# Pair 0 of a pooled attention: rows of maxima through TensorE instead of DMA, k's first rows on ScalarE's queue, one shared last query tile

## The chip, the cores and the metric

The kernel runs on one core of one Trainium2 chip. The metric is the device time of one execution in microseconds (us), as the median of several runs. One execution is an attention followed by two feed-forward layers; the change lies in the first 3% of it.

## The reference, cut to what matters

```python
# q, k, v: (4, 8, 1152, 64) float32
q_pool = q.reshape(B, H, S // 2, 2, D).mean(axis=3)          # 576 query rows per head
scores = scale * np.matmul(q_pool, k.transpose(0, 1, 3, 2))  # 576 x 1152
scores = scores - np.max(scores, axis=-1, keepdims=True)
attn = np.exp(scores)
attn = attn / (np.sum(attn, axis=-1, keepdims=True) + 1e-09)
x = np.matmul(attn, v)                # 32 heads, then laid out as 2304 x 512
h = x @ w_in;  x = (h - np.tanh(h)) @ w_out                  # d_ff 2048
h = x @ w_in2; x = (h / (1.0 + np.exp(-1.702 * h))) @ w_out2
```

## The kernel before, in words

**Pairs and steps.** The 32 heads go in 16 pairs. A pair's two heads lie on partitions 0 to 63 and 64 to 127 of its q and k tiles (64 dimensions each). The main loop counts steps `g`: 9 key tiles of 128 keys for each head, so 18 steps for a pair; steps 0 to 8 belong to head 0 of pair 0, steps 9 to 17 to its head 1, and step 18 opens pair 1. `scores(g)` makes the scores of one key tile, transposed (128 keys by 576 queries, in two PSUM banks), with four matmuls: L400 takes the high part and L401 the correction. For L401 the moving operand `q3` has a 65th row, the negated row of maxima of this head, so that the maximum is subtracted inside the matmul. No scores of a head can start before its `q3` row is there. ScalarE then takes exp of the scores (L406, `pf`), and in two steps of three a second time, rounded (L416, `ph`); VectorE or GpSimd takes their difference (`pl`, L424). `pv(g - 3)` multiplies with v three steps later (L446, six matmuls; in every third step L436, two unrounded ones).

**Maxima.** For a row of maxima, TensorE makes the scores the other way round (128 queries by 1152 keys) only to reduce them: VectorE's `tensor_reduce` leaves one negated maximum per query in a column of `mt`. For the pairs from 1 on, both heads stand in one block-diagonal query tile `bdqs`, and each of nine query tiles is done in two halves of the keys (`max_tile`, L324 and L328), one half in each of 18 steps, starting at step 4 for pair 1. From step 3 on the PSUM pool of these tiles has one buffer. For pair 0 (`first_max`, L340 and L344) head 0's five query tiles (four of 128 rows, one of 64) are done with all 1152 keys at once before the loop, then three of head 1's; head 1's last two tiles follow as halves in steps 0 to 3. `max_rows` (L347) turns the columns of `mt` into a row: a 32x32 transpose on VectorE, then four DMAs (three of SP's queue, one of ScalarE's) into row 64 of `q3`. Head 1's row is made at step 4.

**The opening.** q and k of pair 0 are loaded in halves of 64 partitions (L258, L263: 64 x 1152 float32, 288 KB each), all on SP's queue in the order q low, k low, q high, k high; the third key tiles of v (`prep_v_whole`, 96 KB) go first on ScalarE's queue. VectorE sums the query pairs (L543), ScalarE and GpSimd round k (`k_high`, L551 and L553), GpSimd takes the remainders (`k_low`, L557). `keep_warm` (L585) issues matmuls of zeros whose result nobody reads.

**Order.** The scheduler is off (`tc.manual_schedule`): every engine runs its instructions in the order in which the code issues them. A PSUM pool that closes hands its banks on: the first scores wait for the last reader of the opening's pools. What happens beside the steps is set by tables: `max_at` gives the maxima's steps, `opening` the work of the first pairs by (pair offset, step): `refill_v`, `refill_row` (L234, L238: fixed rows of ones and zeros copied to the second buffer set), `prep_kh`, `prep_bdq`, `prep_qh` (ScalarE), `prep_kl` (GpSimd), `stack` (six DMAs).

Of the kernel before, what the change touches and what calls it, by code (L numbers as in the profile page):

```python
# [28 lines left out]
def tile_pooled_attention_two_moe(  # L29
# [181 lines left out]
    def attention(ctx: ExitStack):  # L211
# [119 lines left out]
        def first_max(s, j, x, pool, parts, n):  # L331
            d = pairs[0]
            r = slice(64 * s, 64 * s + 64)
            a1, _, q2, _ = stacks[0]
            lhs, rhs = (q2, a1) if s == 0 else (d["qh"], d["kh"])
            m = min(128, SP - 128 * j)
            mx = pool.tile([128, parts, 512], F32, tag="mx", name="mx")
            for a in range(parts):
# [4 lines left out]
            c = 16 * x + 5 * s + j
            nc.vector.tensor_reduce(  # L344
                d["mt"][0:m, c:c + 1], mx[0:m, :, 0:n], AX.XY, ALU.max, negate=True)

        def max_rows(p, s, queues=(nc.sync,) * 4):  # L347
# [13 lines left out]
            for a in range(4):  # L361
                if p == 0:
                    m, j = a, 5 * s
                else:
                    j = 0 if s == 0 else 4 if a >= 2 else 5
                    m = 4 * j + a - 18 * s
# [181 lines left out]
        def k_high(eng, out, r, x):  # L548
            o, i = half(out, r, x), half(kraw[0], r, x)
            if eng is nc.scalar:  # L550
                eng.activation(o, i, AF.Copy)  # L551
            else:
                eng.tensor_scalar(  # L553
                    out=o, in0=i, scalar1=1.0, scalar2=1.0, op0=ALU.mult, op1=ALU.mult)
# [14 lines left out]
        nc.scalar.activation(q2[high], d0["qs"][low], AF.Copy)  # L569
        k_high(nc.scalar, d0["kh"], high, 0)  # L570
        k_high(nc.scalar, d0["kh"], high, 1)
        refill_v(1)
        nc.scalar.activation(d0["qh"][high], d0["qs"][high], AF.Copy)
        refill_row(1)
# [341 lines left out]
```

## Time and profile before

| | us |
|---|---|
| median of 3 runs | 1306.44 (1306.07 to 1310.09) |
| the profiled execution, its own time | 1304.36 |
| its span in the profile | 1302.6 |
| TensorE busy in the span | 1286.1 (99%) |
| VectorE, ScalarE, GpSimd busy | 990.2 (76%), 752.7 (58%), 361.9 (28%) |

The span is what the profile covers; 1.76 us of the execution's own time lie outside of it. TensorE is busy nearly throughout, but its busy time in the opening includes the matmuls of zeros, so the opening has to be read row by row: when a row starts, how long it takes, and what released it.

### The profile page before, as it was taken

The numbers are of one execution on the slowest core, as the hardware profiler recorded it, in microseconds if no ns is written. First come the engines' busy times: TensorE is split into PE (matmuls) and PEld (weight loads), VectorE is DVE, ScalarE is ACT, GpSimd is POOL, SyncE is SP. The second block draws the span as 40 slices with busy tenths as digits, with TensorE's granted clock in tenths as the row PEclk, the third lists the DMA queues.
The fourth block names the chain that finished last, engine by engine and source line by source line (L and its number), as shares of the span: only waits on it lengthen the run. The fifth ranks groups of instructions, "written<-read, shape, count | busy, mean of one in ns | idle before, by whom it ended". The sixth has DMA issues, their size and how long they took to land.

```text
span 1302.6 us, 18879 instructions
## 1 busy us (share of the span) xinstructions
PE 1286.1 (99%) x7027; PEld 1148.7 (88%) x7027; DVE 990.2 (76%) x1278; ACT 752.7 (58%) x1153; POOL 361.9 (28%) x272
## 2 busy tenths in 40 slices
PE   8999999999999999999999999999999999999998
PEld 5999999999999998878889889889889889889887
DVE  7777787887878888999999999999943645645433
ACT  5777777777777777776766665665543322322211
POOL 6533333333434333234333332332100100100000
PEclk9999999999999999999999999999999999999999
DMA  6776666676766630211111111111211111111012
GB/s 180 184 177 172 168 168 155 166 186 167 176 167 171 146 89 23 74 49 33 50 33 49 49 33 48 34 33 49 66 36 46 49 33 50 49 33 33 25 41 81
DMA packets 58682, 116.24 MB, mean 89 GB/s; under 512 B 24928, under 2 KB 29024, under 8 KB 58592
## 3 DMA queue, kind: packets, MB, share of 16 engines
q1 hardware_dynamic: 58172, 114.96, 34.1%
q8 instruction: 55, 0.90, 0.3%
q14 instruction: 35, 0.29, 0.1%
q10 hardware_dynamic: 420, 0.10, 0.0%
HBM read 66.58 MB, written 4.79 MB: 55 GB/s over the span
## 4 chain that ended last, share of the span: by engine, by line
PE 81%; DVE 12%; ACT 3%; issue 2%; DMA 1%; POOL 1%; DVEq 0%; SPq 0%; ACTq 0%; POOLq 0%
PE y L802 25%; PE h L707 23%; PE pv L446 10%; PE pv L436 6%; PE mx L324 5%; PE sc L401 5%; PE sc L400 5%; DVE wt L137 1%; DVE gg L765 1%; DVE mt L328 1%; DVE wt L143 1%; DVE mt L344 1%; DVE wt L157 1%; DVE xb L815 1%; DVE wt L150 1%
## 5 line engine op out<-in xcount | busy, mean ns | idle before, releaser
L328 DVE TENSOR_REDUCE mt<-mx 128x1 fp32r<-128x576 f32 x270 | 203.6, 754 | 81.4 <-PE mx L324 77.1
L406 ACT ACTIVATE pf<-sc 128x576 f32<-128x576 f32 x288 | 188.4, 655 | 124.8 <-PE sc L401 110.3
L707 PE MATMUL h<-hl,big 128*128 128x512 f32 (+1 forms) x940 | 211.6, 377 | 0.0
L707 PEld LDWEIGHTS h<-hl,big 128*128 128x128 f32 x940 | 174.0, 188 | 28.6
L400 PE MATMUL sc<-q,big 128*128 128x288 f32 x576 | 183.4, 332 | 0.8 <-DVE mt L344 0.7
L802 PE MATMUL y<-g,big 128*128 128x512 f32 (+1 forms) x780 | 176.6, 369 | 3.3 <-ACT xb L813 1.7
L802 PE MATMUL y<-big,g 128*128 128x512 f32 x702 | 172.2, 390 | 0.0
L802 PEld LDWEIGHTS y<-g,big 128*128 128x128 f32 x780 | 141.9, 188 | 25.0 <-POOL g L719 3.4
L401 PE MATMUL sc<-q,a 65*128 65x288 f32 x576 | 163.7, 298 | 0.0
L719 POOL TENSOR_TENSOR g<-gg,g 128x1024 fp32r<-128x1024 f32 (+1 forms) x39 | 85.8, 2200 | 273.0 <-ACT g L717 273.0
L717 ACT ACTIVATE g<-gg 128x1024 fp32r<-128x1024 f32 (+1 forms) x80 | 78.0, 974 | 140.5 <-DVE gg L778 74.8
L802 PEld LDWEIGHTS y<-big,g 128*128 128x128 f32 x702 | 131.6, 188 | 27.2
L446 PE MATMUL pv<-ph,big 128*128 128x288 f32 x768 | 141.7, 295 | 0.5 <-ACT u L452 0.5
L815 DVE TENSOR_TENSOR xb<-xb,y 128x512 f32<-128x512 f32 (+1 forms) x114 | 72.2, 655 | 87.3 <-PE y L802 87.3
L424 DVE TENSOR_TENSOR pl<-pf,ph 128x576 fp32r<-128x576 f32 x159 | 132.5, 834 | 2.2 <-ACT ph L416 1.5
L707 PE MATMUL h<-hl,w 128*128 128x512 f32 (+1 forms) x564 | 127.0, 377 | 0.0
L165 POOL TENSOR_TENSOR big<-wt,big 128x512 fp32r<-128x512 f32 x46 | 65.2, 1424 | 217.5 <-ACT big L164 217.5
L416 ACT ACTIVATE ph<-sc 128x576 fp32r<-128x576 f32 x188 | 122.8, 653 | 0.0
L707 PEld LDWEIGHTS h<-hl,w 128*128 128x128 f32 x564 | 104.4, 188 | 17.1
L324 PE MATMUL mx<-kh,big 128*128 128x288 f32 x540 | 117.4, 299 | 1.6 <-DVE mt L328 1.4
L446 PEld LDWEIGHTS pv<-ph,big 128*128 128x128 f32 x768 | 116.1, 188 | 1.0 <-issue 0.9
L400 PEld LDWEIGHTS sc<-q,big 128*128 128x128 f32 x576 | 109.3, 190 | 7.1 <-POOL big L385 1.1
(101 smaller groups left out, 2146.5 us busy)
## 6 DMA issues: line engine op xcount, KB each, us to landing
raw<-in_moe_w_in_dram SPq DMA_DIRECT2D x32, 512.0 KB
raw<-in_moe_w_out_dram SPq DMA_DIRECT2D x32, 512.0 KB
big<-kh SPq DMA_DIRECT2D x31, 288.0 KB
q<-qh SPq DMA_DIRECT2D x62, 144.0 KB
big<-kl SPq DMA_DIRECT2D x31, 288.0 KB
a<-kh SPq DMA_DIRECT2D x31, 288.0 KB
kr<-in_k_dram SPq DMA_DIRECT2D x15, 576.0 KB
qr<-in_q_dram SPq DMA_DIRECT2D x15, 576.0 KB
```

What stands on the lines that cost most here:

```text
L324: nc.tensor.matmul(mx[:, a, 0:n], bdqs[p % 2][:, 128 * j:128 * j + 128], d["kh"][:, k0:k0 + n], start=True, stop=True)
L328: nc.vector.tensor_reduce(d["mt"][:, c:c + 1], mx[:, :, 0:n], AX.XY, ALU.max, negate=True)
L400: nc.tensor.matmul(sc[:, x, 0:HB], a1[:, ks], q2[:, xs], start=True, stop=False)
L401: nc.tensor.matmul(sc[:, x, 0:HB], a2[:, ks], q3[:, xs], start=False, stop=True)
L406: nc.scalar.activation(both(pf), sc[:, :, 0:HB], AF.Exp, scale=SCALE)
L416: nc.scalar.activation(both(ph), sc[:, :, 0:HB], AF.Exp, scale=SCALE)
L424: eng.tensor_tensor(pl, pf, f32(ph[:]), op=ALU.subtract)
L446: nc.tensor.matmul(accs[hd][x], w[:, t, :], r[:, x * HB:(x + 1) * HB], start=(t == 0 and n == 0), stop=(t == KT - 1 and n == 2))
L707: nc.tensor.matmul(hb[:, j, 0:TBS[b]], wi[:, c, w, :], x[r][c], start=(k == 0), stop=(k == 3 * NKC - 1))
L719: eng.tensor_tensor(gt[:, :, 1, :], g, f32(gt[:, :, 0, :]), op=ALU.subtract)
L802: nc.tensor.matmul(ys[m][:, 0:w], lhsT, rhs, start=(fp == 0 and k == 0), stop=(fp == 1 and k == 5))
L815: nc.vector.tensor_add(dst, dst, ys[m][:, 0:w])
```

## The change

Pair 0 alone is changed.

- `first_max` writes its maxima into spare columns of `bdqs[0]` (`first_mt`) instead of `mt`. `first_row` makes the row with five matmuls against an identity (which GpSimd writes with `affine_select` into `bdqs[0]`), into the PSUM tile of the zeros (`warm`); ScalarE copies 512 elements of it to `q3`, VectorE the last 64. No transposes and no DMAs are left for pair 0's rows.
- Head 1's and head 0's last 64 queries share one tile of 128 (j = 4), through the block-diagonal `bdqs[1]` and both heads' `kh`.
- Before the loop stand head 0's five tiles, its row, and one half tile of head 1; head 1's other seven half tiles go to steps 0 (two) to 5, its row to step 6 (`second_row`).
- k low is issued on ScalarE's queue; `prep_v_whole` comes after it there.
- Pair 1's first eight half tiles move from steps 4 to 11 to steps 6, 7, 8, 8, 9, 10, 11, 11; where a step has two jobs, the second stands behind the step's `pv`.
- Half of a1's rounding goes from GpSimd to VectorE, `q3`'s remainder (`q_low`) from VectorE to GpSimd. `kh` gets its low half too, for the shared tile.
- `prep_kh` of pair 1, `refill_row` and `refill_v` go from before the loop into steps 1 to 8; `prep_kl`, `sum_q`, `prep_bdq`, `prep_qh`, `prep_ql` and `stack` of pair 1 move one to three steps back.
- `keep_warm` issues 7 + 4 matmuls instead of 11 + 5 + 7.

```diff
-        def refill_v(i):
-            for old, new in zip((*vt[0], vfs[0]), (*vt[i], vfs[i])):
-                nc.scalar.activation(new[:, :, D:128], old[:, :, D:128], AF.Copy)
+        def refill_v(i, n):
+            old, new = [(*vt[x], vfs[x])[n] for x in (0, i)]
+            nc.scalar.activation(new[:, :, D:128], old[:, :, D:128], AF.Copy)
...
+        ident = bdqs[0][:, 0:128]
+        first_mt = bdqs[0][:, 128:288]
+
+        def first_max(s, j, x, pool, parts, n, banks=2):
             d = pairs[0]
+            a1, _, q2, _ = stacks[0]
             r = slice(64 * s, 64 * s + 64)
-            a1, _, q2, _ = stacks[0]
             lhs, rhs = (q2, a1) if s == 0 else (d["qh"], d["kh"])
-            m = min(128, SP - 128 * j)
-            mx = pool.tile([128, parts, 512], F32, tag="mx", name="mx")
+            q0 = 128 * j
+            if j == 4:
+                r, lhs, rhs, q0 = slice(0, 128), bdqs[1], d["kh"], 512
+            mx = pool.tile([128, banks, 512], F32, tag="mx", name="mx")
...
+            c = 64 + 16 * x + 5 * s + j
+            return lambda: nc.vector.tensor_reduce(
+                first_mt[:, c:c + 1], mx[:, 0:parts, 0:n], AX.XY, ALU.max, negate=True)
+
+        def first_row(s, row, js):
+            q3 = stacks[s][3]
+            for j in js:
+                c = 4 if j == 4 else 5 * s + j
+                nc.tensor.matmul(
+                    row[:, 128 * j:128 * j + 128], first_mt[:, c:c + 128], ident,
                     start=True, stop=True)
...
+            if 3 in js:
+                nc.scalar.activation(q3[D:D + 1, 0:512], row[D:D + 1, 0:512], AF.Copy)
+            if 4 in js:
+                nc.vector.tensor_copy(
+                    q3[D:D + 1, 512:SP], row[D:D + 1, 512 + 64 * s:SP + 64 * s])
+
+        def second_row():
+            nc.vector.tensor_tensor(
+                first_mt[:, 69:73], f32(first_mt[:, 69:73]), f32(first_mt[:, 85:89]), op=ALU.min)
+            first_row(1, flat(ps_mx.tile([128, 2, 512], F32, tag="mx", name="mx")), range(5))
...
         load_q(0, low)
-        load_k(0, low)
+        load_k(0, low, nc.scalar)
         load_q(0, high)
+        prep_v_whole(0, 0, nc.scalar)
         load_k(0, high)
         load_v(0, 0)
-        prep_v_whole(0, 0, nc.scalar)
...
         nc.gpsimd.memset(f32(bdqs[0][:]), 0.0)
+        nc.gpsimd.affine_select(
+            out=ident, in_=f32(ident), compare_op=ALU.not_equal, fill=1.0, base=0,
+            pattern=[[-1, 128]], channel_multiplier=1)
...
         q_sum(nc.vector, q2[low], low)
-        k_high(nc.scalar, a1, low, 0)
-        k_high(nc.gpsimd, a1, low, 1)
+        k_high(a1, low, 0)
+        nc.vector.tensor_copy(half(a1, low, 1), half(kraw[0], low, 1))
         q_sum(nc.vector, d0["qs"][low], low)
-        nc.vector.tensor_sub(q3[low], d0["qs"][low], f32(q2[low]))
         k_low(a1, high, low, a1, 0)
+        q_sum(nc.gpsimd, d0["qs"][high], high)
         k_low(a1, high, low, a1, 1)
-        q_sum(nc.gpsimd, d0["qs"][high], high)
+        q_low(q3, low, q2)
+        k_high(d0["kh"], low, 0)
+        k_high(d0["kh"], low, 1)
+        nc.scalar.activation(q2[high], d0["qs"][low], AF.Copy)
+        k_high(d0["kh"], high, 0)
+        k_high(d0["kh"], high, 1)
...
-            keep_warm(11)
-            for j in range(5):
-                first_max(0, j, 0, ps_first, 3, 384)
+            keep_warm(7)
+            for j in range(4):
+                first_max(0, j, 0, ps_first, 3, 384, 3)()
                 keep_warm(1)
-            new_pair(1)
-            max_rows(0, 0, (nc.sync, nc.scalar, nc.sync, nc.sync))
-            for j in range(3):
-                first_max(1, j, 0, ps_first, 3, 384)
-                keep_warm((1, 2, 4)[j])
-        prep_kh(1, 0)
-        prep_kh(1, 1)
+            first_max(0, 4, 0, ps_first, 3, 384, 3)()
+            first_row(0, flat(warm), range(4))
+            reduce = first_max(1, 0, 0, ps_first, 2, HB, 3)
+            first_row(0, flat(warm), range(4, 5))
+            reduce()
...
-        for h in range(4):
-            max_at.setdefault(h, []).append(
-                lambda h=h: first_max(1, 3 + h // 2, h % 2, ps_mx, 2, HB))
+        for h, g in zip(range(1, 8), (0, 0, 1, 2, 3, 4, 5), strict=True):
+            max_at.setdefault(g, []).append(
+                lambda h=h: first_max(1, h // 2, h % 2, ps_mx, 2, HB)())
+        max_at[6] = [second_row]
         for n in range(1, NPAIR):
             for h in range(2 * QJ):
-                max_at.setdefault(NS * n - 14 + h, []).append(
-                    lambda n=n, h=h: max_tile(n, *divmod(h, 2)))
+                g = NS * n - 14 + h
+                if h < 8 and n == 1:
+                    g = (6, 7, 8, 8, 9, 10, 11, 11)[h]
+                max_at.setdefault(g, []).append(lambda n=n, h=h: max_tile(n, *divmod(h, 2)))
...
-            (0, 4): [(max_rows, 1, (nc.sync, nc.scalar, nc.sync, nc.sync))],
-            (1, 1): [(sum_q,)], (1, 2): [(prep_bdq, 0)], (1, 3): [(prep_bdq, 1), (prep_qh,)],
-            (2, 1): [(load_q,)], (1, 4): [(prep_ql,)],
-            (1, 5): [(stack, 0)], (1, 8): [(prep_v, 0)], (1, 10): [(stack, 1)],
+            (0, 1): [(lambda p: prep_kh(1, 0),)], (0, 2): [(lambda p: prep_kh(1, 1),)],
+            (0, 4): [(lambda p: refill_row(1),)], (0, 5): [(lambda p: refill_v(1, 0),)],
+            (0, 7): [(lambda p: refill_v(1, 1),)],
+            (0, 8): [(lambda p: refill_v(1, 2),),
+                     (lambda p: nc.gpsimd.memset(f32(bdqs[0][:, 0:288]), 0.0),)],
+            (0, 9): [(lambda p: fill(2),)],
+            (1, 3): [(sum_q,), (prep_kl, 0)], (1, 4): [(prep_bdq, 0), (prep_kl, 1)],
+            (1, 5): [(prep_bdq, 1), (prep_qh,)],
+            (2, 1): [(load_q,)], (1, 6): [(prep_ql,)],
+            (1, 7): [(stack, 0)], (1, 8): [(prep_v, 0)], (1, 10): [(stack, 1)],
...
-            for job in max_at.get(g, ()):
+            two = max_at.get(g, ())
+            for job in two[:1] if g >= LAG else two:
                 job()
             if 0 < g <= total:
                 rest(g - 1)
             if g >= LAG:
                 pv(g - LAG)
+                for job in two[1:]:
+                    job()
```

**TensorE, from the last tile of maxima to the first scores.** Rows in brackets name the semaphores that an instruction waits for. Before (L340 maxima, L585 zeros, L400 and L401 scores):

```order
L585 MATMUL warm<-big 128x512 x2
L340 MATMUL mx<-kh,qh 128x384 [waits DVE_49]
L340 MATMUL mx<-kh,qh 128x384 x2
L585 MATMUL warm<-big 128x512 x4
L400 MATMUL sc<-q_0_79,big 128x288 [waits DVE_49,PE_49,Pool_49]
L401 MATMUL sc<-q_0_80,a_0_78 128x288 [waits DMAHW2_49,DMAHW3_49,DMAHW1_49,DMAHW0_49]
```

And now (L345 maxima, L355 the row's matmuls, L415 and L416 scores):

```order
L345 MATMUL mx<-kh,big 128x384 [waits DVE_49,Activation_49]
L345 MATMUL mx<-kh,big 128x384 x2
L355 MATMUL warm<-big 128x128 [waits DVE_49,Pool_49]
L355 MATMUL warm<-big 128x128 x3
L345 MATMUL mx<-kh,qh 128x288 [waits PE_49,Activation_49]
L345 MATMUL mx<-kh,qh 128x288
L355 MATMUL warm<-big 128x128 [waits Activation_49]
L415 MATMUL sc<-q_0_79,big 128x288 [waits DVE_49,PE_49,Pool_49]
L416 MATMUL sc<-q_0_80,a_0_78 128x288 [waits Pool_49]
```

The four waits for DMAs are gone; waits for VectorE, ScalarE and again VectorE stand between the last tile and the first scores. The zeros in between are gone too.

**ScalarE, steps 4 to 6 of head 0.** Before (L406 `pf`, L416 `ph`, L295 and L287 rounding of pair 1's queries, L369 the DMA of head 1's row):

```order
L295 ACTIVATE big<-qs 64x576
L287 ACTIVATE qh<-qs 128x576
L406 ACTIVATE pf<-sc 128x576
L369 DMA q_1_83<-tt 1x5x32
L406 ACTIVATE pf<-sc 128x576
L416 ACTIVATE ph<-sc 128x576
L406 ACTIVATE pf<-sc 128x576
L416 ACTIVATE ph<-sc 128x576
```

And now (L421 `pf`, L431 `ph`, L238 `refill_row`, L234 `refill_v`, L359 the copy of head 1's row):

```order
L421 ACTIVATE pf<-sc 128x576
L238 ACTIVATE a_1_81<-a_0_78 1x1152
L295 ACTIVATE big<-qs 64x576
L421 ACTIVATE pf<-sc 128x576
L431 ACTIVATE ph<-sc 128x576
L234 ACTIVATE big<-big 128x9x64
L295 ACTIVATE big<-qs 64x576
L287 ACTIVATE qh<-qs 128x576
L421 ACTIVATE pf<-sc 128x576
L431 ACTIVATE ph<-sc 128x576
L359 ACTIVATE q_1_83<-mx 1x512
```

Five copies and roundings now stand between step 4's `pf` and step 6's `pf`, and the copy of the row behind that.

**TensorE, two tiles of pair 1's maxima (L324) in a row.** Before, with a step between them:

```order
L324 MATMUL mx<-kh,big 128x288 x2
L436 MATMUL pv_319<-pf,rbd 128x288
L436 MATMUL pv_320<-pf,rbd 128x288
L400 MATMUL sc<-q_0_79,big 128x288
L401 MATMUL sc<-q_0_80,a_0_78 128x288
L400 MATMUL sc<-q_0_79,big 128x288
L401 MATMUL sc<-q_0_80,a_0_78 128x288
L324 MATMUL mx<-kh,big 128x288 x2
```

And now, from the end of step 8 to step 9:

```order
L324 MATMUL mx<-kh,big 128x288 x2
L415 MATMUL sc<-q_1_82,big 128x288
L416 MATMUL sc<-q_1_83,a_1_81 128x288
L415 MATMUL sc<-q_1_82,big 128x288
L416 MATMUL sc<-q_1_83,a_1_81 128x288
L324 MATMUL mx<-kh,big 128x288 x2
```

Only four matmuls of scores stand between the two tiles, which share one PSUM buffer.

## Rows read from the trace of the kernel before

**Rows 1.** The page: span and part 1, busy us of each engine.

```profile
span 1302.6 us, 18879 instructions
...
PE 1286.1 (99%) x7027; PEld 1148.7 (88%) x7027; DVE 990.2 (76%) x1278; ACT 752.7 (58%) x1153; POOL 361.9 (28%) x272
```

**Rows 2.** Busy time by stretch; PEclk is the granted clock's share.

```profile
core 0: us, PE busy (x) PEld busy (x) DVE busy (x) ACT busy (x) POOL busy (x), PEclk, DMA share, GB/s
18.87:40.66 21.79, 19.47 (x121) 16.93 (x121) 16.36 (x22) 14.04 (x24) 10.35 (x11) 1.00 0.94 233
40.66:60.00 19.34, 19.30 (x131) 18.15 (x130) 14.86 (x23) 14.97 (x28) 11.54 (x9) 1.00 0.87 216
```

**Rows 3.** Timeline of TensorE: start, us, instructions [idle before, releaser].

```profile
2.12 4.54 PE L585 MATMUL warm<-big 128*128 128x512 f32 x11 [2.12 <-DVE big L230]
...
16.97 1.19 PE L585 MATMUL warm<-big 128*128 128x512 f32 x4
18.87 0.37 PE L400 MATMUL sc<-q,big 128*128 128x288 f32 x1 [0.71 <-DVE mt L344]
19.11 0.37 PE L401 MATMUL sc<-q,a 65*128 65x288 f32 x1
...
24.25 0.47 PE L340 MATMUL mx<-kh,qh 64*64 64x288 f32 x2 [0.97 <-DVE mt L344]
...
30.98 0.54 PE L324 MATMUL mx<-kh,big 128*128 128x288 f32 x2 [1.35 <-DVE mt L328]
...
32.69 0.43 PE L324 MATMUL mx<-kh,big 128*128 128x288 f32 x2
...
35.53 0.29 PE L400 MATMUL sc<-q,big 128*128 128x288 f32 x1
...
40.66 0.29 PE L400 MATMUL sc<-q,big 128*128 128x288 f32 x1
```

**Rows 4.** Timeline of VectorE.

```profile
4.63 0.75 DVE L543 TENSOR_TENSOR q<-qr 64x576 fp32r<-64x576 f32 x1 [2.49 <-DMA qr<-in_q_dram]
...
8.08 6.41 DVE L344 TENSOR_REDUCE mt<-mx 128x1 fp32r<-128x1152 f32 x5 [1.24 <-PE mx L340]
...
14.84 3.89 DVE L344 TENSOR_REDUCE mt<-mx 128x1 fp32r<-128x1152 f32 x3
...
27.99 1.38 DVE L356 TENSOR_TENSOR mt<-mt 128x2 fp32r<-128x2 f32 x1
...
33.16 0.76 DVE L328 TENSOR_REDUCE mt<-mx 128x1 fp32r<-128x576 f32 x1 [0.84 <-PE mx L324]
...
44.65 0.16 DVE L353 TENSOR_TENSOR mt<-mt 128x5 fp32r<-128x5 f32 x1
```

**Rows 5.** Timeline of GpSimd.

```profile
7.45 2.79 POOL L557 TENSOR_TENSOR big<-kr,big 64x576 fp32r<-64x576 f32 x2
...
25.89 3.46 POOL L304 TENSOR_TENSOR kl<-kr,kh 128x576 fp32r<-128x576 f32 x2 [6.78 <-DMA big<-kl]
```

**Rows 6.** Timeline of ScalarE and of SP's queue.

```profile
6.12 0.69 ACT L551 ACTIVATE big<-kr 64x576 fp32r<-64x576 f32 x1 [3.64 <-DMA kr<-in_k_dram]
...
12.34 1.14 ACT L238 ACTIVATE a<-a 1x1152 fp32r<-1x1152 f32 x1
...
14.76 2.17 SPq L369 DMA_DIRECT2D q<-tt  x3
...
16.36 1.26 ACT L300 ACTIVATE kh<-kr 128x576 fp32r<-128x576 f32 x2 [2.87 <-DVE mt L344]
...
26.04 0.69 ACT L287 ACTIVATE qh<-qs 128x576 fp32r<-128x576 f32 x1
26.64 0.63 ACT L406 ACTIVATE pf<-sc 128x576 f32<-128x576 f32 x1
...
30.99 0.65 ACT L416 ACTIVATE ph<-sc 128x576 fp32r<-128x576 f32 x1
31.52 0.66 ACT L406 ACTIVATE pf<-sc 128x576 f32<-128x576 f32 x1
```

More of the change, by code (lines that the diff above doesn't have):

```diff
@@ L258, in load_q, with load_k @@
             nc.sync.dma_start(out=qraw[p][rows], in_=q[p // NPB, p % NPB][rows])
-        def load_k(p, rows=slice(0, 128)):
+        def load_k(p, rows=slice(0, 128), queue=nc.sync):
             if p not in kraw:
                 kraw[p] = ap.tile([128, S], F32, tag="kr", name="kr", bufs=2)
-            nc.sync.dma_start(out=kraw[p][rows], in_=k[p // NPB, p % NPB][rows])
+            queue.dma_start(out=kraw[p][rows], in_=k[p // NPB, p % NPB][rows])
         def load_v(p, s):
@@ L340, in first_max, with max_rows @@
                 nc.tensor.matmul(
-                    mx[0:m, a, 0:n], lhs[r, 128 * j:128 * j + m], rhs[r, k0:k0 + n],
-                    start=True, stop=True)
[L343 to L347, printed above, removed]
+                    mx[:, a, 0:n], lhs[r, q0:q0 + 128], rhs[r, k0:k0 + n], start=True, stop=True)
+            c = 64 + 16 * x + 5 * s + j
[7 more added lines that the diff above has]
+                    row[:, 128 * j:128 * j + 128], first_mt[:, c:c + 128], ident,
+                    start=True, stop=True)
+            if 3 in js:
[7 more added lines that the diff above has]
+            first_row(1, flat(ps_mx.tile([128, 2, 512], F32, tag="mx", name="mx")), range(5))
+        def max_rows(p, s):
             d = pairs[p]
@@ L361, in max_rows @@
             for a in range(4):
[L362 to L366, printed above, removed]
+                j = 0 if s == 0 else 4 if a >= 2 else 5
+                m = 4 * j + a - 18 * s
                 n = len(range(m, SP // 32, 4))
                 g = 32 * a + j
-                queues[a].dma_start(
+                nc.sync.dma_start(
                     out=row[:, m:SP // 32:4, :], in_=f32(tt[g:g + n, :]))
@@ L546, in half, with k_high @@
             return t[r, x * SP:(x + 1) * SP]
[L548 to L554, printed above, removed]
+        def k_high(out, r, x):
+            nc.scalar.activation(half(out, r, x), half(kraw[0], r, x), AF.Copy)
         def k_low(out, to, r, hi, x):
@@ L558, in k_low, with q_low @@
                 half(out, to, x), half(kraw[0], r, x), f32(half(hi, r, x)), op=ALU.subtract)
+        def q_low(out, r, hi):
+            nc.gpsimd.tensor_tensor(out[r], d0["qs"][r], f32(hi[r]), op=ALU.subtract)
         q_sum(nc.vector, q2[low], low)
[L561 to L562 removed]
+        k_high(a1, low, 0)
+        nc.vector.tensor_copy(half(a1, low, 1), half(kraw[0], low, 1))
         q_sum(nc.vector, d0["qs"][low], low)
[L564 removed]
         k_low(a1, high, low, a1, 0)
+        q_sum(nc.gpsimd, d0["qs"][high], high)
         k_low(a1, high, low, a1, 1)
[L567 to L578 removed]
+        q_low(q3, low, q2)
[4 more added lines that the diff above has]
+        k_high(d0["kh"], high, 1)
+        nc.scalar.activation(bdqs[1][low, 512:SP], d0["qs"][low, 512:SP], AF.Copy)
+        nc.scalar.activation(bdqs[1][high, SP:640], d0["qs"][high, 512:SP], AF.Copy)
+        nc.scalar.activation(d0["qh"][high], d0["qs"][high], AF.Copy)
+        nc.scalar.activation(a2[low], kraw[0][low], AF.Copy)
         with (tc.tile_pool(name="ps_warm", bufs=1, space=PSUM) as ps_warm,
@@ L604, in attention @@
         load_v(1, 1)
-        prep_kl(1, 0)
-        prep_kl(1, 1)
         load_k(2)
-        fill(2)
         ps_sc = ctx.enter_context(tc.tile_pool(name="ps_sc", bufs=2, space=PSUM))
```

19 lines of the change are left out of this document (7 added, 12 removed).

## The prediction

> **What bounds the kernel now.** First the page: TensorE is busy for 1286.1 of 1302.6 us [rows 1], so only time in which TensorE waits can be won. The stretches say where it is: from 40.66 us on TensorE has work for 19.30 of 19.34 us, while the 21.79 us before that, which begin with the first scores at 18.87, hold 2.3 us of idling [rows 2], and nothing before 18.87 is a matmul of the main loop. So the question is at what time TensorE reaches the scores of step 12 (40.66 us before [rows 3]) with the same work behind it; from there on the two kernels have the same order but for one wait. Third, TensorE's timeline: the first scores were released by VectorE's reduction, 0.71 us after the last zeros, and the first L401, which also waits for the row's DMAs, follows at 19.11 with no idling of its own [rows 3]. **The DMAs of the row bound nothing**: they were issued from 14.76 on [rows 6] and landed under head 1's three reductions, which began at 14.84 and took 3.89 us [rows 4]. What the change can win at the start is therefore those three reductions ahead of the first scores, less what takes their place.
>
> **The start, part by part.** *Loads.* k low landed for ScalarE at 6.12 behind 96 KB of v and q low's 288 KB [rows 6]; q low was used from 4.63 on [rows 4]. Now the two halves start at once on two queues and v comes behind them. If the bytes flow as before, 96 KB fewer at the 233 GB/s of the later stretch [rows 2] bring k low to 5.7 us; q low shares the way and comes at 5.7 too, at most 1.1 us later than before. I take 5.7 for both; ends 5.3 and 6.1.
>
> *First tile.* VectorE has the query sum (0.75 [rows 4]), the new copy of half of a1 and the second sum (0.75) to do before the first reduction. The copy has no row: it lies between half a sum, 0.35, and a whole one, 0.75. So the first reduction could start at 5.7 + 0.75 + 0.35 + 0.75 = 7.55, or at 7.95. But GpSimd's remainder of a1 (2.79 / 2 = 1.40 [rows 5]) becomes ready 0.75 after k low, at 6.45, between VectorE's copy and its second sum. What such a meeting costs is in the trace: a minimum of two columns took 1.38 us while GpSimd had its pair of differences from 25.89 to 29.35, against 0.16 when alone [rows 4, 5]; it ended with GpSimd's. The sum would then wait to 7.85 and end at 8.6. I take 8.3 for the first reduction (8.08 before), with the ends 7.5 and 8.8. [...]
>
> *Five reductions*: 6.41 us as before [rows 4], the last tile now for both heads: to 14.7 (13.9 to 15.2).
>
> *The row.* Five 128-column matmuls, of which no row exists; two matmuls of 288 columns take 0.43 and one 0.29, so they follow each other by 0.14 [rows 3], and the first four take between 0.3 and 0.7 with their latency, say 0.6; ScalarE's 512 elements from PSUM on one partition 0.6, as its 576-column operations do (0.65 [rows 6]; 0.5 to 0.7, since 1152 elements of one partition took 1.14); the fifth matmul 0.3; VectorE's 64 elements 0.2 (0.16 for five columns); four handovers of 0.05 to 0.14. That is 2.0 us (1.6 to 2.6). Then head 1's first half tile, 0.76 on VectorE, which the first scores wait for since it lies in the pool that closes, and 0.14 to wake TensorE: 2.9 in all. **First scores at 17.6 instead of 18.87** (16.4 to 18.5): 1.25 us won (0.4 to 2.5). GpSimd's later work (remainders, v) and ScalarE's a2 are due only then; four to five GpSimd operations of 1.4 fit between 8.6 and 17.
>
> **From the first scores to step 12.** Let S be the first scores. *ScalarE.* Its pace is 0.53 for an exp (30.99 to 31.52) and 0.60 to 0.63 for a rounding (26.04 to 26.64; 1.26 for two) [rows 6]. Before step 4's `pf` come seven exps and two `prep_kh`, formerly done while ScalarE idled (2.87 us before them): 7 x 0.53 + 2 x 0.6 = 4.9, from S + 0.75 on, so step 4's `pf` starts at S + 5.65. From it to the end of the copy of head 1's row: five exps 2.65, `refill_row` 1.14, four roundings 2.4 and the copy 0.5 make 6.7: the copy ends at S + 12.4. If TensorE is held at step 3, as it was by 0.97 us at 24.25, or VectorE's minimum of four columns meets GpSimd's difference as L356 did, at S + 13.4. Behind the copy stands pair 1's first half tile, since the row and the tiles share the one PSUM buffer. TensorE itself has only about 9.5 us of work up to there, so it idles 3 us.
>
> *TensorE from that tile to step 12.* Three steps with a half tile each took 40.66 - 35.53 = 5.13, steps 9 to 11, without pause [rows 3]. Steps 7 to 11 are five: 8.55, and three half tiles more (0.27 each) 0.8: 9.35. But two tiles that share the buffer can't follow each other faster than matmuls 0.47 (32.69 to 33.16), reduction 0.76 and 0.14: 1.37 us [rows 3, 4]. Between them there is now sometimes only sc (four matmuls, 0.54) and the tile's own 0.27, which leaves 0.56 to wait (steps 6 to 7, 8 to 9, 11 to 12), or only `pv` (six, 0.8) and the 0.27, which leaves 0.3 (within 8 and 11): 1.7 up to step 12 and 0.56 more behind its scores. So step 12 starts at S + 12.4 + 9.35 + 1.7 = S + 23.4 (to S + 24.5) where it was S + 21.79: **2.2 to 3.3 us lost, with the last wait; I take 2.9.**
>
> **The sum.** 2.9 - 1.25 = 1.65 us longer (ends 0.3 shorter and 2.9 longer, with both uncertain costs at their ends on the same side). Made against the profiled execution's 1304.36, that is 1306.0; the median of the runs lies 2.08 above it, so 1306.44 + 1.65 = 1308.1. 0.3% is 3.9 us, about what a measurement of this kernel can tell from no change, so this reads as no change.
>
> **Rivals.** *1. The start is kept.* If nothing holds TensorE ahead of the copy and the doubled tiles find their buffer free, step 12 starts at S + 12.4 + 9.35 = S + 21.75, as far behind the first scores as before; with those at 17.3 that gives 1306.44 - 1.55 = 1304.9. For it: VectorE has less to reduce for head 1, eight halves of 0.76 (6.1) instead of three whole tiles and four halves (3.89 + 3.0). Against it: the 1.37 us of a shared buffer are three rows in a chain, and the order leaves 0.81 or 1.07 of work beside them.
>
> [...]
>
> *3. Waits behind GpSimd add up (slower).* Its queue is full from 6.5 to some 20 us and then has `prep_kl` (3.46 [rows 5]), which meets VectorE's `pl` and the sum of pair 1's queries on the way to head 1's last tiles; `affine_select`, without a row (0.3 to 2), stands ahead of all of it. Two meetings of 1.2 us on the path that ends at the copy, beyond the one counted, give 1310.5.
>
> *4. The start is worth more than I see* (a first reduction before 7 us, a row in 1 us, no ScalarE queue): 1302, over 0.3% faster. Nothing in the rows supports it.
>
> **How the numbers follow.** Forecast 1308.1: 0.57. Rival 1: 0.18. Rival 2: 0.10. Rival 3: 0.11. Rival 4: 0.04. Faster by over 0.3%: rival 4, 0.04; slower by over 0.3%: rivals 2 and 3, 0.21; within: 0.75. The range leaves out rival 4 and the upper half of 2 and 3, and holds rival 1: 1304.5 to 1311.
>
> **What would show it.** In the changed kernel's trace: the first reduction (L348) at 8.3 and the second sum of queries stretched beside GpSimd; first scores (L415) at 17.6, released by VectorE; the first copy to `q3` (L359) some 1.5 us before them, the second ending 12.4 to 13.4 us after them, behind an unbroken row of ScalarE's work; TensorE's first L324 released by ScalarE, the next ones waiting 0.3 and 0.56 for VectorE; step 12's scores at 41.7. If the first L324 comes before S + 11, the ScalarE step is wrong; if TensorE's waits after 20 us sum to less than 3 us, the loss is.

## The result: slower, at half pace

The changed kernel takes 1316.86 us (median of 6 runs, 1315.32 to 1317.07) against 1306.26 for the kernel before beside it: ratio 1.0064, 95% interval 1.0049 to 1.0080. (The quotient of these two medians is 1.0081. The kernel before spreads from 1303.88 to 1310.09 in six runs; its medians over 25 to 35 executions, below, were 1308.4 to 1309.7.) The forecast was 1308.1, in a range from 1304.5 to 1311; "slower by over 0.3%" had 0.21. The profiled span is 1315.2 us, 12.6 above [rows 1].

The changed kernel's page, span and part 1, against [rows 1]:

```profile
span 1315.2 us, 18867 instructions
...
PE 1297.0 (99%) x7024; PEld 1157.7 (88%) x7024; DVE 989.3 (75%) x1279; ACT 755.5 (57%) x1159; POOL 362.4 (28%) x274
```

TensorE is busy for 10.9 us more with three instructions fewer: its matmuls became longer. Its timeline (columns as in [rows 3]; the zeros are now L599, tiles of pair 0 L345, the row L355, scores L415):

```profile
2.12 3.36 PE L599 MATMUL warm<-big 128*128 128x512 f32 x7 [2.12 <-DVE big L230]
7.09 1.33 PE L345 MATMUL mx<-big,q 64*128 64x384 f32 x3 [1.62 <-ACT big L567]
...
17.58 1.08 PE L355 MATMUL warm<-big 128*128 128x128 f32 x4 [1.54 <-POOL kl L570]
...
21.03 0.58 PE L415 MATMUL sc<-q,big 128*128 128x288 f32 x1 [1.18 <-DVE big L348]
...
41.84 0.53 PE L324 MATMUL mx<-kh,big 128*128 128x288 f32 x2
...
52.86 0.29 PE L415 MATMUL sc<-q,big 128*128 128x288 f32 x1
```

Step 12's scores start at 52.86, not 40.66 [rows 3]. Until 41 us nearly every matmul takes up to twice its time (scores follow each other by 0.24 us from 21.40 on, by 0.13 to 0.14 from 42.20 on); then it has the old one back: L324 at 41.84 takes 0.53, as one took 0.54 at 30.98 before [rows 3]. Yet the granted clock hides this. Windows of the changed kernel:

```profile
core 0: us, PE busy (x) PEld busy (x) DVE busy (x) ACT busy (x) POOL busy (x), PEclk, DMA share, GB/s
...
25.00:30.00 5.00, 4.99 (x15) 3.53 (x16) 3.41 (x4) 3.92 (x7) 2.67 (x2) 1.00 0.33 117
...
55.00:60.00 5.00, 5.00 (x36) 4.79 (x35) 3.25 (x7) 4.38 (x8) 1.92 (x2) 1.00 0.03 11
```

TensorE is full in both, with 15 matmuls in one and 36 in the other, at a column of 1.00 in both: **in this trace, in which the pace is low from the first matmul on, the column doesn't show it; the count does.** Three of the six executions read 1.00 in the mean, the other three 0.987 or 0.988, and all take 1315.3 to 1317.1 us. VectorE's and ScalarE's starts:

```profile
5.16 0.75 DVE L561 TENSOR_TENSOR q<-qr 64x576 fp32r<-64x576 f32 x1 [3.01 <-DMA qr<-in_q_dram]
6.36 0.45 DVE L578 CAST big<-kr 64x576 fp32r<-64x576 f32 x1 [0.45 <-DMA kr<-in_k_dram]
6.73 0.74 DVE L561 TENSOR_TENSOR qs<-qr 64x576 f32<-64x576 f32 x1
8.53 1.36 DVE L348 TENSOR_REDUCE big<-mx 128x1 fp32r<-128x1152 f32 x1 [1.05 <-PE mx L345]
```

```profile
41.20 0.59 ACT L359 ACTIVATE q<-mx 1x512 fp32r<-1x512 f32 x1
```

The first reduction comes at 8.53 (forecast 8.3), the second row's copy ends 20.8 us behind the first scores (forecast 12.4 to 13.4).

### The profile page after: what moved, and what is told of

The parts are those of the page before. It is cut to its first block, busy times and chain, and to the rows that moved or that the text cites. A ratio compares the mean times of both kernels' runs of the same rounds, so it can differ in the third digit from the quotient of the medians.

```text
span 1315.2 us, 18867 instructions
## 1 busy us (share of the span) xinstructions
PE 1297.0 (99%) x7024; PEld 1157.7 (88%) x7024; DVE 989.3 (75%) x1279; ACT 755.5 (57%) x1159; POOL 362.4 (28%) x274
## 4 chain that ended last, share of the span: by engine, by line
PE 85%; DVE 7%; ACT 2%; issue 2%; POOL 1%; DMA 1%; DVEq 0%; POOLq 0%; ACTq 0%
PE y L827 27%; PE h L732 25%; PE pv L461 10%; PE pv L451 7%; PE sc L415 5%; PE sc L416 5%; PE mx L324 5%; DVE mt L328 1%; DVE gg L790 1%; DVE wt L143 1%; DVE wt L137 1%; DMA big<-kh 1%; DVE wt L157 1%; ACT u L771 1%; DVE wt L150 0%
## 5 line engine op out<-in xcount | busy, mean ns | idle before, releaser
L421 ACT ACTIVATE pf<-sc 128x576 f32<-128x576 f32 x288 | 188.5, 655 | 131.1 <-PE sc L416 120.7
L415 PE MATMUL sc<-q,big 128*128 128x288 f32 x576 | 186.2, 336 | 1.3 <-DVE big L348 1.2
L416 PE MATMUL sc<-q,a 65*128 65x288 f32 x576 | 165.7, 301 | 0.0
L431 ACT ACTIVATE ph<-sc 128x576 fp32r<-128x576 f32 x188 | 122.8, 653 | 0.0
L324 PE MATMUL mx<-kh,big 128*128 128x288 f32 x540 | 117.7, 300 | 1.2 <-DVE mt L328 0.9
L415 PEld LDWEIGHTS sc<-q,big 128*128 128x128 f32 x576 | 111.2, 193 | 7.7 <-POOL big L403 1.3
```

Source lines behind the costliest of these rows:

```text
L324: nc.tensor.matmul(mx[:, a, 0:n], bdqs[p % 2][:, 128 * j:128 * j + 128], d["kh"][:, k0:k0 + n], start=True, stop=True)
L415: nc.tensor.matmul(sc[:, x, 0:HB], a1[:, ks], q2[:, xs], start=True, stop=False)
L416: nc.tensor.matmul(sc[:, x, 0:HB], a2[:, ks], q3[:, xs], start=False, stop=True)
L421: nc.scalar.activation(both(pf), sc[:, :, 0:HB], AF.Exp, scale=SCALE)
L431: nc.scalar.activation(both(ph), sc[:, :, 0:HB], AF.Exp, scale=SCALE)
```

## Experiments: is it the clock, and what holds it

Each timed run has 10 to 12 executions of its kernel beside 25 to 35 of the kernel before, whose medians were 1308.4 to 1309.7; ratios and intervals are against those. "Zeros" are the matmuls of `keep_warm`.

**e1.** Eleven zeros, as before.

```
-            keep_warm(7)
+            keep_warm(11)
```

> The changed kernel with eleven matmuls of zeros ahead of the first tile, as before, instead of seven; nothing else differs. Theory A (clock, set at the start): the array is at half pace because it worked too little before the first tile and then waited 1.6 us. With eleven zeros the wait is about 0.4 us; the tiles of maxima run at 0.16 instead of 0.24 to 0.31 per 288 to 384 columns, five reductions follow each other by 1.28 instead of 1.98, first scores at 17.5 to 18 instead of 21.03, scores of step 12 at 41 to 43 instead of 52.86; 1305 to 1309 us. Theory B (clock, set by the pauses of the row): the first tiles are fast, but the 1.5 us pause ahead of the row and the 1.2 us ahead of the scores bring half pace back; step 12 at 47 to 51; 1311 to 1315 us. Theory C (no clock: the granted clock reads 1.00 throughout; the matmuls are slow for what they read or wait for): 1315 to 1318 us as the changed kernel.

1314.31 us, 1.0034 [1.0017, 1.0051]; step 12 at 49.72. That is theory B. Windows and timeline of e1:

```profile
10.00:15.00 5.00, 3.04 (x12) 1.91 (x12) 4.25 (x4) 2.88 (x6) 4.72 (x5) 0.85 0.98 257
15.00:20.00 5.00, 3.82 (x14) 2.99 (x13) 1.03 (x3) 1.36 (x3) 4.83 (x5) 0.50 0.41 87
```

```profile
11.87 0.76 PE L345 MATMUL mx<-kh,big 128*128 128x384 f32 x3
14.39 1.09 PE L355 MATMUL warm<-big 128*128 128x128 f32 x4 [1.76 <-DVE big L348]
```

Here the record has a fall, and the column shows it: three matmuls in 0.76 at 11.87, 1.76 us of waiting for the row's maxima, then four of 128 columns in 1.09 (0.56 in e9, at full pace). First scores came at 17.84 (forecast 17.6).

**e2.** The kernel before with seven zeros.

```
-            keep_warm(11)
+            keep_warm(7)
```

> The kernel before with seven matmuls of zeros instead of eleven; nothing else differs. Theory A (clock, set at the start): the pause ahead of the first tile grows from 0.2 to 1.8 us, the tiles and the scores run at half pace for some twenty us or more; first scores at 21 to 23 instead of 18.87 and step 12 8 to 12 us later than 40.66; 1313 to 1319 us. Theory B (pauses of the row) and theory C (no clock): the order of the kernel before has no such pauses, the main loop runs as before and only the first tiles change; 1305 to 1308 us.

1313.74 us, 1.0034 [1.0014, 1.0053]: theory A. First scores came at 24.24 instead of 18.87 (expected 21 to 23). Without four of its zeros the kernel before takes 4.6 us more.

**e3 and e4.** Four zeros ahead of the row, with seven or eleven at the start.

```
+            keep_warm(4)
             first_row(0, flat(warm), range(4))
```

> The changed kernel (seven zeros at the start) with four matmuls of zeros put between the last tile of head 0 and the row, where TensorE waits 1.5 us. Theory A (clock, set at the start): the start is slow as in the changed kernel, and the zeros shorten the half pace a little at most: full pace from 35 to 41 us instead of 41; 1313 to 1317 us. Theory B (the pause ahead of the row keeps it at half pace): full pace from about 21 us on, step 12 at 44 to 46; 1307 to 1310 us. Theory C: 1316 to 1318 us.

> Eleven zeros at the start and four ahead of the row, in the changed kernel. Theory A (start alone): the same as with eleven alone, within 0.5 us, since four zeros at full pace take 0.9 us inside a wait; 1305 to 1309 us. Theory B (both pauses matter): full pace throughout, 1305 to 1309 us, and 4 to 8 us better than with eleven alone. Theory C: 1316 to 1318 us.

1316.67 and 1313.58 us (1.0048 and 1.0033). e3's time lies in theory A's range, but its traced execution, the fastest of ten, had full pace at the first tile, with seven zeros and a wait of 1.21 us, which A excludes; e4's time is in no theory's range. e4's tiles and row are at full pace, and it fell at 18.0, behind the waits of 0.83 and 1.18 us that were left. In e3 full pace came, went at 9.6, came again at 16.4 and went at 19.8.

**e5, e6, e7, e8.** Waits filled with matmuls: in the changed kernel those ahead of the row and of the scores (e5, below), in the kernel before the one ahead of the scores (e6: seven zeros for four; e7: also `fill_pause(g, {3: 5, 6: 8}[g])`, matmuls of 288 columns into the next scores' tile at steps 3 and 6). e8 is the kernel before again, for its trace.

```
+            keep_warm(8)
             first_row(0, flat(warm), range(4))
...
+            keep_warm(5, ps_first.tile([128, 3, 512], F32, tag="mx", name="mx")[:, 0])
```

> The changed kernel with TensorE kept busy up to the first scores: eleven zeros at the start, eight ahead of the row, five between the row's last matmul and the scores. Theory D, formed on the first four runs (pauses of TensorE before the first scores let the clock fall, 0.8 us being enough in one run, and it then takes about 20 us of work to come back): no fall before the scores, first scores at 17.8 to 18.3, scores of step 12 at 41 to 43 instead of 49.7 to 52.9; profiled span 1303 to 1306, median 1304 to 1309 us. Rival E (the clock falls by the moment at which the chip looks, or by the lighter main loop, whatever the pauses): it falls all the same, at some place between 15 and 30 us; median 1312 to 1315.

> The kernel before with seven instead of four zeros ahead of the first scores, where TensorE waits 0.71 us; nothing else differs. The kernel before has spans of 1302.1 to 1312.3 us in these runs, most of them 1306 to 1308 with a granted clock of 0.992, which says that in most executions some 20 us go at half pace. Theory D: if this pause is what lets the clock fall, most executions now come at a clock of 1.00 and spans of 1302 to 1303; median 1304 to 1305 against 1307 to 1309. If the pauses of 0.97 and 1.35 us inside the main loop do it, no change: 1306 to 1309.

> The kernel before with seven zeros ahead of the first scores and with five and eight matmuls of 288 columns, whose result is overwritten, in TensorE's waits of 0.97 us at step 3 and of 1.35 us at step 6. Theory D: no fall at all, nearly all executions at a clock of 1.00, spans 1301.5 to 1303.5, median 1303 to 1305. Rival E: spans spread from 1302 to 1312 as before, median 1306 to 1309.

> The kernel before as it is, once more, for its trace: four of five executions show a granted clock below 1.00, the one profiled so far did not. Theory D: if this one does, the fall lies within a few us behind one of the pauses at 18.2, 23.3 or 29.6 us, and the pace comes back about 20 us later; span 1306 to 1310. Rival E: it falls in a stretch in which TensorE had no pause.

1310.64 (1.0010 [0.9996, 1.0024]), 1306.88 (0.9990 [0.9973, 1.0008]), 1311.30 (1.0015 [1.0003, 1.0028]) and one run of 1311.23. Theory D falls with e8, which lost its clock at 13.3 us with no such wait, and e6 with it, at 14.9 behind waits of 0.20 at most. e5 doesn't decide: it fell at 10.0 us, 2 us behind a wait of 1.05 ahead of the first tile that its zeros had left. In e7 the matmuls at step 3 were followed by a wait of 2.23 us (0.97 in [rows 3]) and a second fall. Timeline and windows of e8, the unchanged kernel before:

```profile
11.90 0.72 PE L340 MATMUL mx<-big,q 64*64 64x384 f32 x3
12.55 0.49 PE L585 MATMUL warm<-big 128*128 128x512 f32 x1
13.26 1.22 PE L340 MATMUL mx<-kh,qh 64*128 64x384 f32 x3 [0.21 <-DVE mt L344]
...
20.97 0.58 PE L400 MATMUL sc<-q,big 128*128 128x288 f32 x1
```

```profile
10.00:15.00 5.00, 4.74 (x15) 2.37 (x13) 4.86 (x6) 3.57 (x6) 4.93 (x5) 0.83 0.10 36
15.00:20.00 5.00, 5.00 (x12) 3.15 (x12) 3.54 (x3) 1.26 (x2) 3.96 (x5) 0.50 0.40 108
```

TensorE reads 4.74 of 5 busy, its longest wait is 0.21 us, and still it fell. One tile and one zero per reduction is all that it has there: thin work, which its busy time doesn't show. The trace of [rows 3], with waits of 0.19 to 0.26 us in the same stretch, kept its clock. **The kernel before loses its clock in most executions:** of the 29 beside the last runs two had spans of 1302.1 and 1302.2 at a clock of 1.00, 24 had 1306.2 to 1312.9 at 0.988 to 0.993 (three lay between). The trace that the prediction read was one of the few.

**e9, e10, e11.** More work: thirteen (e10: twelve) zeros at the start and three behind each tile; e9 and e11 with e5's others, e10 with seven ahead of the scores; e11 also copies head 1's row on VectorE.

```
-                keep_warm(1)
+                keep_warm(3)
...
+                if s == 0:
                     nc.scalar.activation(out, i, AF.Copy)
+                else:
+                    nc.vector.tensor_copy(out, i)
```

> The changed kernel with thirteen zeros at the start, three instead of one behind each of the first four tiles, eight ahead of the row and five ahead of the scores. The kernel before fell to half pace at 13.3 us in the last run although its idle times there are 0.21 us at most: a tile's matmuls and one matmul of zeros were all that TensorE had between two reductions. Theory F (the clock falls where TensorE's work is thin, whether the profile shows it idle or not): with three zeros per tile it does not fall before the scores; first scores at 17.6 to 18.3, scores of step 12 at 41 to 43; spans 1303.5 to 1306.5, median 1305.5 to 1308 against 1310.64 with one zero per tile. Rival E (the moment at which the chip looks decides): spans and clocks spread as with one zero per tile, 1306 to 1310; median 1309 to 1312, or worse by the 1.7 us that eight more zeros take at half pace.

> The kernel before with twelve zeros at the start, three behind each of the first seven tiles and seven behind the eighth, instead of eleven, one, one, two and four. Theory F: it does not fall ahead of the scores; spans mostly 1302 to 1304 with a clock of 0.998 to 1.00, median 1304 to 1305.5 where the kernel before gives 1307 to 1309. Rival E: spans of 1302 to 1312 as before, median 1306 to 1310.

> The changed kernel with the zeros as in the first of these three runs, and with the 512 columns of head 1's row copied by VectorE instead of ScalarE. The prediction's ScalarE step: the copy stands behind an unbroken row of exps and roundings, ended 14.2 us after the first scores, and TensorE waited 1.84 us for it. By that step the copy now ends right behind VectorE's minimum, some 11.5 to 12 us after the first scores, the wait of 1.84 us is gone, step 12 comes 1.5 to 2.5 us earlier, and with it the time, more where the wait let the clock fall: 1302.5 to 1305.5 us. Rival: TensorE or VectorE holds the row there anyway, the time is the same as with ScalarE's copy within 0.7 us.

1310.83 (1.0015 [1.0001, 1.0029]), 1307.72 (0.9985 [0.9972, 0.9998]) and 1307.47 (0.9986 [0.9976, 0.9997]). As theory F has it, none of the three traces has a fall ahead of the scores, and no execution of e10 is below 0.997. The times were missed: a tile with three zeros takes 1.61 us, over the reduction's 1.36, and first scores came at 19.77, 20.76 and 19.20. e9 fell later, behind one wait; e9, then e11:

```profile
34.03 0.72 PE L324 MATMUL mx<-kh,big 128*128 128x288 f32 x2 [1.84 <-ACT q L359]
34.56 0.44 PE L415 MATMUL sc<-q,big 128*128 128x288 f32 x1
```

```profile
31.80 0.51 PE L324 MATMUL mx<-kh,big 128*128 128x288 f32 x2 [0.16 <-ACT qh L287]
...
42.81 0.29 PE L419 MATMUL sc<-q,big 128*128 128x288 f32 x1
```

The second pair's first half tile stands 14.26 us behind the first scores with ScalarE's copy, and 12.60 with VectorE's: the copy's place costs 1.66 us, and in the median 3.4: all ten executions of e9 read below 1.00 (0.995 to 0.999), seven of e11's ten 1.00.

**e12 to e15.** Starting from e11: two zeros per tile, six and four (e12); the second pair's half tiles at steps 6, 7, 8 and so on, its row of maxima at step 15 for 13 (e13); both (e14); e12 with k on SyncE's queue (e15).

```
-                keep_warm(3)
+                keep_warm(2)
...
-                    g = (6, 7, 8, 8, 9, 10, 11, 11)[h]
+                    g = 6 + h
...
-        load_k(0, low, nc.scalar)
+        load_k(0, low)
```

> The kernel with VectorE's copy of head 1's row and many zeros, with fewer of them: two instead of three behind each tile, six instead of eight ahead of the row, four instead of five ahead of the scores. With three, TensorE's own matmuls (1.61 us a tile) held VectorE's reductions (1.36 us) back. Theory G (the zeros' price is only the later first scores, and two per tile are work enough for full pace): first scores at 17.8 to 18.1 instead of 19.20, the rest as it was; median 1305.7 to 1306.6 against 1307.47. Rival H (two are too few): the clock falls ahead of the scores in some executions, spans from 1303 to 1310, median 1307.5 to 1310.

> The kernel with VectorE's copy and many zeros (1307.47 us, step 12 at 23.61 us behind the first scores where the kernel before had 21.79), with the second pair's ten half tiles of maxima one to a step at steps 6 to 15 instead of eight of them within steps 6 to 11, two of these steps holding two, and its row of maxima at step 15 instead of 13. The prediction's step of the shared buffer (waits of 0.3 to 0.56 for VectorE's reduction where two tiles follow closely, 1.7 us up to step 12 and 0.56 behind it): the waits of 0.31 and 0.32 at the L324 go, step 12 comes 1.0 to 1.8 us earlier behind the first scores, and the median falls to 1305.7 to 1306.7. Rival (the waits are hidden later): the time stays at 1307 to 1308, or rises where the row of step 18 then waits for its transfers.

> Both: fewer zeros and one half tile to a step. Theory G with the step of the shared buffer: the two gains add up, 1304 to 1305.5 us, below the kernel before by 2 to 4 us. Rivals as with each alone: 1307 to 1310.

> The kernel with VectorE's copy and fewer zeros, with k's first rows loaded from SyncE's queue again, between the two halves of q, as before the change; v stays behind on ScalarE's. The prediction's step of the loads (both halves land at 5.7 with two queues; the second queue brings 0.2 to 0.4 us at most): first reduction within 0.5 us of its time with two queues, the same median within 0.5 us. Rival (the second queue is what brings the start forward): the first reduction and the first scores come 0.6 to 1.2 us later, and the time with them.

1306.62 (0.9989 [0.9974, 1.0005]), 1309.52 (1.0013 [0.9998, 1.0028]), 1308.87 (1.0010 [0.9995, 1.0026]) and 1307.14 us (0.9992 [0.9976, 1.0008]). e12: first scores at 17.52; four of 12 executions read 0.996 or 0.997. The one traced fell at 22.85, behind waits of 0.25 us at most (the same two matmuls take 0.53 at full pace, in e11):

```profile
22.39 0.53 PE L345 MATMUL mx<-kh,qh 64*128 64x288 f32 x2 [0.25 <-DVE big L348]
22.85 0.85 PE L465 MATMUL pv<-ph,big 128*128 128x288 f32 x2
```

e13 did what was expected up to step 12, 21.87 us behind the first scores instead of 23.61, and gave more back later, in two places. First, the tiles at steps 14 and 15 push the row's work into GpSimd's. VectorE and GpSimd of e13:

```profile
48.90 1.79 DVE L291 TENSOR_TENSOR ql<-qs,qh 128x576 fp32r<-128x576 f32 x1
```

```profile
48.67 3.29 POOL L304 TENSOR_TENSOR kl<-kr,kh 128x576 fp32r<-128x576 f32 x2
```

A VectorE subtraction that took 0.75 at 33.38 in the same run takes 1.79 beside GpSimd's, and TensorE then waits 0.90 for VectorE at 51.41; from step 12 to the copy of the second head's output it is 16.90 us, 15.71 in e11. Second, the doubling wasn't taken away but moved. The edit shifts all 18 half tiles of the second pair, to steps 6 to 23, and at steps 22 and 23 stand the third pair's first two already. From the scores of step 22 to those of step 25, e13, then e11:

```profile
59.72 0.30 PE L419 MATMUL sc<-q,big 128*128 128x288 f32 x1
...
61.84 0.53 PE L324 MATMUL mx<-kh,big 128*128 128x288 f32 x2 [0.18 <-DVE mt L328]
...
67.14 0.29 PE L419 MATMUL sc<-q,big 128*128 128x288 f32 x1
```

```profile
59.90 0.29 PE L419 MATMUL sc<-q,big 128*128 128x288 f32 x1
...
64.87 0.29 PE L419 MATMUL sc<-q,big 128*128 128x288 f32 x1
```

7.42 us against 4.97: two doubled steps cost 2.45 us there. e14 has both losses too (waits of 0.90 at 50.05, 0.18 and 0.32 at 60.48 and 61.86). A schedule without any doubled step was not run. e15: VectorE's start, e15, then e12:

```profile
4.79 0.75 DVE L565 TENSOR_TENSOR q<-qr 64x576 fp32r<-64x576 f32 x1 [2.64 <-DMA qr<-in_q_dram]
6.11 0.45 DVE L582 CAST big<-kr 64x576 fp32r<-64x576 f32 x1 [0.57 <-DMA kr<-in_k_dram]
```

```profile
4.83 0.75 DVE L565 TENSOR_TENSOR q<-qr 64x576 fp32r<-64x576 f32 x1 [2.69 <-DMA qr<-in_q_dram]
6.12 0.45 DVE L582 CAST big<-kr 64x576 fp32r<-64x576 f32 x1 [0.55 <-DMA kr<-in_k_dram]
```

In these two traces the second queue brings nothing. With two queues it can also cost: in e4, e5, e9, e13 and e18 k landed first and q last, at 6.43 to 6.80 us, and the first reduction started at 8.65 to 9.04 (7.75 in e15, 8.08 in [rows 4]).

**e18, e16, e17.** The changed kernel with e12's zeros and nothing else altered; the kernel before with thirteen at the start, two per tile and five ahead of the scores; the same with four and six matmuls in the main loop's waits.

```
-            keep_warm(11)
+            keep_warm(13)
...
-                keep_warm((1, 2, 4)[j])
+                keep_warm((2, 2, 5)[j])
```

> The changed kernel with nothing altered but its zeros: thirteen at the start, two behind each of four tiles, six ahead of the row, four ahead of the scores. It is what the forecast of 1308.1 us was made for: the start at full pace and the ScalarE copy of head 1's row. The forecast's steps: first scores at 17.4 to 18.2, the copy 14.2 us behind them with a wait of 1.8 us of TensorE (measured with more zeros; forecast 12.4 to 13.4 and 3 us), step 12 at 25.0 to 25.5 us behind the first scores; 1307.5 to 1309.5 us, below the changed kernel by 7 to 9 us, and 1.0 to 2.5 us above the same kernel with VectorE's copy. If the half pace were not the cause of the difference to the forecast, it would stay above 1312.

> The kernel before with thirteen zeros at the start, two behind each of the first seven tiles of maxima and five behind the eighth, instead of eleven, one, one, two and four. Theory F (thin work ahead of the scores lets the clock fall in most executions of the kernel before, at 13.3 us in the one that was traced): first scores at 18.9 to 19.4, no fall ahead of them; spans mostly 1303 to 1304.5, falls only behind the pauses of the main loop; median 1305.5 to 1307 against 1308.5 to 1309, and better than with three zeros per tile (1307.72) by the 1.5 us that its scores came later. Rival H: two zeros are too few, falls in a third of the executions or more, 1307.5 to 1309.

> The same, with four and six matmuls of 288 columns in TensorE's waits at steps 3 and 6 of the main loop (0.97 and 1.35 us in the kernel before). If the falls that are left come from these two waits: spans 1302.5 to 1304.5 in nearly all executions, median 1304.5 to 1306, the best of all. If not, the ten matmuls only delay what stands behind them: 1306 to 1308.

e18: 1309.58 us, 0.9999 [0.9985, 1.0013], where the changed kernel had 1.0064 [1.0049, 1.0080]: zeros alone take away 0.65%, 8.5 us (the two medians differ by 7.3). Its traced execution had q last and first scores at 18.62 (expected 17.4 to 18.2), and fell at 22.4, behind waits of 0.23 us at most since 8 us and ahead of the copy's wait, so that the expected 25 us to step 12 can't be read off it. **e16 is the best of all, 1305.54 us, 0.9966 [0.9952, 0.9979]**, with no execution below 0.997; as expected (1305.5 to 1307), though thirteen zeros held its first tile up to 7.96 us and its first scores to 20.16. Its windows:

```profile
10.00:15.00 5.00, 5.00 (x20) 2.48 (x18) 4.93 (x5) 3.46 (x6) 4.92 (x5) 1.00 0.09 32
15.00:20.00 5.00, 4.88 (x19) 2.84 (x18) 4.86 (x5) 1.26 (x2) 3.71 (x5) 1.00 0.14 22
...
25.00:30.00 5.00, 4.38 (x16) 3.86 (x17) 3.65 (x4) 3.70 (x6) 3.04 (x2) 0.54 1.08 257
```

20 and 19 matmuls, and no fall there; what is left falls behind a wait of 1.03 us at 24.6. From its first tile to its fall e8 had 20 matmuls in 6.13 us, the trace of [rows 3] 20 in 6.51 without a fall, e16 25 in 7.02: the count of matmuls alone doesn't tell the trace that fell from the one of [rows 3] that didn't. Which of e16's three additions is needed wasn't tried. e17 kept the clock as well (0.997 to 1.00, no fall in its trace) and was slower, 1307.91 (0.9992 [0.9976, 1.0008]): its matmuls at step 6 write to the next scores' tile, which ScalarE still read.

```profile
32.91 1.06 PE L398 MATMUL sc<-q,big 128*128 128x288 f32 x6 [2.05 <-ACT ph L425]
```

## Why the prediction was wrong, step by step

- *The step that failed: TensorE's pace.* The sum of 1308.1 has no term for it; only rival 2, a TensorE that is slow at the start, stands for it, at +2.5 us and a chance of 0.10. No run shows these 2.5 us: with seven zeros, and longer waits at the start and during the row, the first tile's three matmuls took 1.33 us, against 0.76 to 0.79 for a tile in e1, and the low pace lasts to 41 us. An estimate: at full pace step 12 would stand at about 17.5 (e12's first scores) + 23.6 (e11) + 1.66 (the copy) = 42.8; it stands at 52.86. **About 10.1 of the 12.2 us are pace.** That no wait of the kernel before left a slow matmul behind it [rows 3] held for one execution; e8 is the counterexample.
- *The base.* The 2.08 us by which the median lay above the profiled execution were added as an offset. They are the kernel's own clock losses (beside e16 to e18, 1302.1 us at a column of 1.00, 1306.2 and more at 0.993 and below), and three runs from 1306.07 to 1310.09 hinted at them.
- *Loads:* both halves at 5.7 was wrong. With two queues one is used from 4.65 to 5.34, the other from 5.95 to 6.80, and in five of eleven traces it is q that comes last.
- *First tile:* the copy took 0.45, as bounded. The second sum wasn't stretched (0.74): GpSimd's remainder started at 7.18, behind ScalarE's half. When k lands first, the meeting does happen: e13's first sum, not the second, took 1.18 from 6.51 on, where it takes 0.75 in e12, while GpSimd had 5.66 to 7.08.
- *First scores at 17.6:* held where q landed first (17.84 in e1, 17.52 in e12, 17.41 in e15, 18.22 in e14); with q last e18 has 18.62, outside the range to 18.5.
- *ScalarE's chain:* right in kind, 1.8 us short: in e5 and e9 the half tile stands 14.26 us behind the scores, forecast 12.4 to 13.4, and TensorE waits 1.84, forecast 3, since its steps 0 to 6 take 12.4 us, not 9.5. For the 9.5 no working was given: the kernel before is busy for 9.79 us with 56 matmuls from 18.87 to 30.98, e11 has 70 in that stretch.
- *Half tile to step 12:* forecast 9.35 + 1.7 = 11.05, measured 11.01 in e11; 9.28 in e13, without doubling and with two half tiles fewer (0.27 each). The sum is right by luck: TensorE reads 10.26 us busy and 0.75 idle, where 9.35 and 1.7 were forecast. The waits that show were 0.31 and 0.32.
- *Rival 3:* head 1's minimum meets GpSimd in the changed kernel (1.20 us at 38.02) without a wait of TensorE behind it; at full pace it takes 0.17 (e5, e9, e11).
- *The sum at full pace:* e15's lowest span is 1303.3, that of the kernel before 1302.1, and its profiled one 1302.6; with the copy's 1.66 the change costs 2.4 to 2.9 us by this estimate, forecast 1.65. No run shows it directly. e18's ratio of 0.9999 is against a kernel before that has clock losses of its own: that there is no difference, as was forecast, is luck.
- *That the row's DMAs bound nothing* was not tried by itself.

Open: what decides in which execution a given kernel falls. The moment differs between executions of one kernel, e12 and e18 fell without thin work ahead of the scores and without a long wait, and no run here tells why.

## What to carry to other kernels

Before a change of a start phase is priced, look at the spread of the runs, and at how many matmuls a full stretch holds: a trace of the fastest execution says nothing about the pace of the others. Matmuls that only keep TensorE at work are part of the kernel's design: taking away four of them cost the kernel before 4.6 us, and adding nine in the right places won it 4.2 (1309.73 to 1305.54). Time that a transfer seems to cost at the start should be checked for what releases the next engine; the first scores of the kernel before were released by VectorE [rows 3]. And an edit that moves work out of one place has to be followed to where the work goes: e13's doubled steps came back at steps 22 and 23.

## What the runs showed of the hardware

TensorE fell to half pace behind waits of 1.76 us (e1), 1.84 (e9) and 1.03 (e16), and also where no wait in the ten us before was above 0.25 (e6, e8, e12, e18). Matmuls then took up to twice their time: two of 288 columns 0.85 (e12) instead of 0.53 (e11), four of 128 columns 1.09 (e1) instead of 0.56 (e9). The way back was short in some traces, 7 us (e6, 14.9 to 21.9, with seven zeros at its end; e12, 22.9 to 29.5, in the main loop), and long in others: 20 us (e8, 13.3 to 33.8) and 23 (e1, 14.4 to 37.4). e8's 20 us cost 6.8 us of its span (1309.4 against 1302.6), not 10: of the waits of 0.71, 0.97 and 1.35 us [rows 3] only the second shows, at 1.90 us. The granted clock's column shows a fall only if the record has one: the changed kernel's trace, at half pace to 41 us, reads 1.00.
